# ScalarE's decode steps beside attention keep their place in the queue, at three quarters of the pace

## The chip, the core and the metric

The kernel runs on one core of a Trainium2 chip. The metric is the device time of one execution in microseconds (us). TensorE (PE) multiplies and transposes, and its weight loads (PEld) overlap its matmuls; VectorE (DVE), ScalarE (ACT) and GpSimd (POOL) do elementwise work; SyncE (SP) issues nearly all transfers. Every engine runs its own queue in order: an instruction that waits holds all that stand behind it.

## The reference, cut to what matters

```
x = attention(q, k, v)            # batch 4, heads 8, seq 576, head_dim 64; window of 128, ALiBi bias
x = ((x @ w_a) * (x @ w_b)) @ w_out         # tokens 2304, d_model 512, d_ff 1536
x = f(x @ w_in2) @ w_out2                   # d_ff 2048
# f(h): h if h >= 1; 0 if h <= -1; else (h + 1)**2 / 4
```

q, k and v are 32-bit floats, the five weight matrices 64-bit floats.

## The kernel before

The weights are read as raw 64-bit words in tiles of 128x512 (512 KB) and turned into 32-bit floats on the chip. One such decode is `words` (L518) and a last add: ScalarE writes `e` from the high words (L530) and `up` from the low words (L532); VectorE bounds `e` (L535), shifts it (L539), merges the sign from the high words (L541, the last reader of the raw tile) and adds `up` (L546). There are 68 weight tiles.

Attention runs in rounds. For each block of 64 queries TensorE forms the scores (L348), VectorE reduces them to a maximum (L354), ScalarE takes the exponential (L358), GpSimd normalizes (L363, L369); three rounds later TensorE transposes the probabilities (L380), a copy (mostly ScalarE's, L176) brings them to SBUF as `pt`, and two rounds after that the values are multiplied (L412) and cast into the tiles `x`. Between the rounds TensorE works on the first feed-forward network for half blocks of 256 tokens, with the first four tiles of each weight (gate L593 to L595, down L642).

In the same stretch a third strand decodes 22 more weight tiles ahead of time (`EARLY`): `early_job` (L689) decodes one tile and stores it as 32-bit floats to DRAM (L694, 256 KB), from where it is read back after attention. The main loop at the end of the kernel takes one step of this strand (a job is seven steps) per step of the feed-forward products, `WE` times. The raw words of the coming tiles are loaded by `fetch_next` (L512) until `FETCH` of them are there and unused; there are three raw buffers (two with the tag w64, one w64c). `e` and `up` have two buffers each (`EB`, `UB`), so the first ScalarE step of a job writes into the `e` that the job two before has stored, and waits until that store has landed.

The order in which instructions stand on each engine isn't that of the code. A scheduler goes through the traced program with modelled times and puts each instruction in its engine's queue when the model has its inputs ready. An instruction can be tied to stand behind the one traced just before it on its engine (an order, with no wait on the data).

After attention one visit of the last block of 768 tokens uses the plain weights (L1117, L1148); the other visits use a seven-product form (L1027) on combined weights, that background jobs build from the decoded tiles.

Of the kernel before, what the change touches and what calls it, by code (L numbers as in the profile page):

```python
# [9 lines left out]
F32 = mybir.dt.float32  # L10
# [3 lines left out]
AF = mybir.ActivationFunctionType  # L14
# [12 lines left out]
def attention_and_two_ffns(  # L27
# [12 lines left out]
    nc = tc.nc  # L40
# [53 lines left out]
    YB = 4  # L94
    EARLY = 22
    EFROM = 1
    WE = 1
    HOLD = 3
    PRI = 300
    ET = mybir.EngineType  # L100
# [5 lines left out]
    BG = [(3, 2, 24), (3, 1, 24), (1.5, 1, 19), (2, 1, 12), (3, 1, 0), (3, 1, 0), (2, 1, 0)]  # L106
    VISITS = [(1, 0), (1, 1), (1, 2), (2, 0), (2, 1), (2, 2)]
    FLIP = [0, 1, 0, 0, 1, 0]
    FETCH = 2
    ABS = 'AA'  # L110
    D7 = ((2, 2),)
    GN = 11
# [9 lines left out]
    E_PV = 'V'  # L122
    TQ = 3
    TN = 3
    HP = lambda n: n < HPN
    const = ctx.enter_context(tc.tile_pool(name="const", bufs=1))
    xp = ctx.enter_context(tc.tile_pool(name="xp", bufs=1))
# [41 lines left out]
    def minus(eng, out_, a, hi):  # L169
        eng.tensor_tensor(out_, a, hi.bitcast(F32), ALU.subtract)  # L170
# [298 lines left out]
    def ready(t1):  # L469

        return all(
            t in done for _, t in todo if t[0] * S + PART[int(t[2] >= 2)][0] < t1
        )
# [5 lines left out]
    state = {"w": 0, "credit": 0.0}  # L479
# [24 lines left out]
    def fetch(key, tag="w64"):  # L504
        pool, bw = (later["dec"], WB2) if later else (wdec, WB if tag == "w64" else 1)
        src = source(key)
        raws[key] = raw = pool.tile([P, 4 * P], I64, tag=tag, name="w64", bufs=bw)
        nc.sync.dma_start(
            raw.rearrange("p (c f) -> p c f", f=src.shape[-1]) if len(src.shape) == 3 else raw, src
        )  # L510

    def fetch_next():  # L512

        while coming and len(raws) < FETCH:
            count["e"] = count.get("e", 0) + 1
            fetch(coming.popleft(), "w64" if count["e"] % 3 or FETCH < 2 else "w64c")

    def words(key):  # L518

        pool, be, bu = (later["dec"], EB2, UB2) if later else (wdec, EB, UB)  # L520
        if key not in raws:
            fetch(key)
        raw = raws.pop(key)
        word = raw.bitcast(U32).rearrange("p (n two) -> p n two", two=2)
        lo, hi = word[:, :, 0], word[:, :, 1]
        e = pool.tile([P, 4 * P], U32, tag="e", name="e", bufs=be)
        up = pool.tile([P, 4 * P], U32, tag="up", name="up", bufs=bu)
        ef = e.bitcast(F32)
        if ABS[bool(later)] == "A":
            nc.scalar.activation(ef, hi.bitcast(F32), AF.Abs)  # L530
            yield e, up
        nc.scalar.activation(up, lo, AF.Copy, scale=2.0**-29)  # L532
        yield e, up
        if ABS[bool(later)] == "A":
            nc.vector.tensor_scalar(ef, ef, W64_MIN, W64_MAX, ALU.max, ALU.min)  # L535
        else:
            nc.vector.tensor_scalar(ef, hi.bitcast(F32), W64_MIN, W64_MAX, ALU.abs_max, ALU.min)
        yield e, up
        nc.vector.tensor_scalar(e, e, 5, 2, ALU.logical_shift_left, ALU.logical_shift_right)  # L539
        yield e, up  # L540
        nc.vector.scalar_tensor_tensor(e, hi, 0xC0000000, e, ALU.bitwise_and, ALU.bitwise_or)  # L541
        yield e, up

    def total_bits(dst, e, up):
        shape = (lambda t: t.rearrange("p (a n) -> p a n", a=2)) if len(dst.shape) == 3 else (lambda t: t)
        nc.vector.tensor_tensor(dst, shape(e), shape(up), ALU.add)  # L546

    def w_tile(name):
        return wp.tile([P, 2, 4 * P], F32R, tag="w", name=name)

    def decode(key):
        for e, up in words(key):
            pass
        total_bits(e, e, up)
        t = w_tile("w")
        low = e.bitcast(F32)
        nc.scalar.copy(t[:, 0], low)
        minus(ENG[LESS], t[:, 1], low, t[:, 0])
        wt[key] = t

    def room():
        return WP - state["w"]

    def take(key):
        assert room(), key
        state["w"] += 1

    def give(key):
        state["w"] -= 1

    def pump():
        if not waiting or not room():
            return False
        key = waiting.popleft()
        take(key)
        with tc.high_priority() if HP(order.index(key)) else ExitStack():
            decode(key)
        if not waiting:
            fetch_next()
        return True  # L580
# [95 lines left out]
    V = nc.vector  # L676
# [10 lines left out]
    coming = deque(ahead)  # L687

    def early_job(key):  # L689
        for e, up in words(key):  # L690
            yield
        total_bits(e, e, up)
        early[key] = dram.tile([P, 4 * P], F32, name=f"w32_{key[0]}{key[1]}")
        nc.sync.dma_start(early[key], e.bitcast(F32))  # L694
        fetch_next()
        yield
# [98 lines left out]
    def run(jobs):  # L795

        try:
            return next(jobs[0]) != "no room"
        except StopIteration:
            jobs.popleft()  # L800
            return True
# [24 lines left out]
    less_, plus_ = ALU.subtract, ALU.add  # L826
    def two():
        both = later["dec"].tile([P, 2, QW], F32, tag="x32", name="x32", bufs=1)
        return both[:, 0], both[:, 1]
# [60 lines left out]
    def t_tile(where):  # L890
        if where == "xt":
            return later["xt"].tile([P, 2, 2, QW], F32R, tag="xt", name="xt", bufs=3)
        return xp.tile([P, 2, 2, QW], F32R, tag="x", name="xt", bufs=NB * NC)

    def x_tile(name):
        return xp.tile([P, 2, BW], F32R, tag="x", name=name, bufs=NB * NC)

    def x7_second(b, where):

        t1, t2 = two()  # L900
        xs[b] = [x_tile(f"z{c}") for c in range(NC)]
        if where == "memory":
            parked[2, b] = {q: dram.tile([P, 2, 2, QW], F32, name=f"t2_{b}{q}") for q in (2, 3, 6)}
        else:
            turned[2, b] = {q: t_tile(where) for q in (2, 3, 6)}

        def split(hi, lo, src):
            nc.scalar.copy(hi, src)
            yield
            minus(V, lo, src, hi)  # L910
            yield

        def turn(q, c, src):
            if where != "memory":
                yield from split(*(turned[2, b][q][:, z, c] for z in range(2)), src)
                return
            while not room():
                yield "no room"
            me = ("turned2", b, q, c)
            take(me)  # L920
            t = w_tile("wt")
            yield from split(t[:, 0, :QW], t[:, 1, :QW], src)
            nc.sync.dma_start(parked[2, b][q][:, :, c], t[:, :, :QW].bitcast(F32))
            give(me)

        for c in range(2):
            f = xp.tile([P, 2, BW], F32, tag="x", name="xf", bufs=NB * NC)
            nc.sync.dma_start(f, xf[b][:, c])
            yield
            b11, b12, b21, b22 = f[:, 0, Q1], f[:, 0, Q2], f[:, 1, Q1], f[:, 1, Q2]  # L930
            V.tensor_tensor(t1, b12, b11, less_)
            yield
            V.tensor_tensor(t2, b22, t1, less_)
            yield
            V.tensor_tensor(b12, b22, b12, less_)
            yield
            yield from turn(3, c, t1)
            yield from turn(2, c, t2)
            V.tensor_tensor(t1, b21, t2, less_)
            yield  # L940
            for k in range(2):
                x = xs[b][c + 2 * k]
                yield from split(x[:, 0], x[:, 1], f[:, k])
            yield from turn(6, c, t1)
        made.add((2, b))
        yield
# [475 lines left out]
    def after_attention():  # L1422
# [22 lines left out]
        with tc.manual_schedule(engines=set(MANUAL)) if MANUAL else ExitStack():  # L1445
            for i, v in enumerate(visits):
# [13 lines left out]
                if here == (2, 1):  # L1460
                    jobs_x.append(x7_second(2, "xt"))
                for f in v["fs"]:
                    final = f == v["fs"][-1]

                    def hook(q):
# [8 lines left out]
                        if D7 and here == (2, 1):  # L1474
                            if q == TQ and f != visits[-1]["fs"][-1]:
                                turns[f] = turn_job(v, f)
                            for z in sorted(turns)[:1] if FLIP[i - 1] == 0 else sorted(turns)[::-1][:1]:
                                for _ in range(TN):
                                    if next(turns[z], "end") == "end":
# [43 lines left out]
    for need in products():  # L1523
        if need is not None:
            begun += 1
            while not later and (need > NT or not ready(need)):
                step()
                steps += 1
                if steps % PUMP[0] == PUMP[1]:
                    pump()  # L1530
        if not later and begun >= 0:
            for _ in range(XE):
                if jobs_x:
                    run(jobs_x)
            if begun >= EFROM and ahead and not waiting and not jobs_w:
                jobs_w.append(early_job(ahead.pop(0)))
            for _ in range(WE):
                if jobs_w:
                    run(jobs_w)
        owed += PACE[min(begun, len(PACE) - 1)]  # L1540
        while owed >= 1.0:
            owed -= 1.0
            step()
# [30 lines left out]
```

## Time and profile before

| | us |
|---|---|
| median of three runs | 975.7 (973.14 to 975.98) |
| the profiled execution | 974.94 |
| its span, first to last instruction | 973.2 |
| PE busy in the span | 937.1 (96%) |
| DVE, ACT, POOL busy | 720.6, 565.0, 169.5 |
| decodes ahead of time: ScalarE's first step of the first and of the last | 84.8 and 203.0 |
| TensorE's last product of attention values ends | about 243 |

The busy shares are averages over stages with different limits, so the table only says that TensorE is the engine to look at. Where it stood idle or ran at a lower granted clock is read from the stretches of time, and what it waited for from the waits and the timeline of the same stretch.

### The profile page before, as it was taken

To read this page: it belongs to the slowest core of one execution; us is meant where nothing else is said; L and a number is where in the kernel's file an instruction comes from. 1 tells how busy PE (TensorE), PEld (TensorE's weight loads), DVE (VectorE), ACT (ScalarE), POOL (GpSimd) and SP (SyncE) were. 2 spreads that over 40 slices of the span, in tenths; PEclk is the share of its full clock that TensorE was granted. 3 is DMA by queue.
4 is the path that set the end of the run, shared out by engine and by line. 5 is a ranking of instruction groups with operands and counts; after the bars stand their busy time and mean duration, and the time that the engine had idled before them with its cause. 6 is when DMAs were issued, how large, how long until landed. Compare 5 with 4: busy or idle time off the path is not lost.

```text
span 973.2 us, 18277 instructions
## 1 busy us (share of the span) xinstructions
PE 937.1 (96%) x6397; PEld 874.6 (90%) x6397; DVE 720.6 (74%) x1704; ACT 565.0 (58%) x1346; POOL 169.5 (17%) x311
## 2 busy tenths in 40 slices
PE   4999999899999999999999999999999999999997
PEld 3889889799999899999989999888888888899997
DVE  6698787794944988885677667899876656467886
ACT  6778676664433454353434435788775656586662
POOL 5567444344100000000000000000000000032233
PEclk9999999999999999999999999999999999999999
DMA  9967787830545888798868997876777776587851
GB/s 215 181 147 180 209 218 185 220 98 2 163 156 198 311 311 301 281 365 332 265 225 328 383 364 271 310 247 211 272 285 238 246 241 229 178 269 257 268 185 65
DMA packets 177580, 229.01 MB, mean 235 GB/s; under 512 B 92880, under 2 KB 132048, under 8 KB 177488
## 3 DMA queue, kind: packets, MB, share of 16 engines
q1 hardware_dynamic: 173680, 224.96, 70.9%
q10 hardware_dynamic: 3808, 2.88, 1.0%
q8 instruction: 51, 0.84, 0.3%
q14 instruction: 41, 0.34, 0.1%
HBM read 156.24 MB, written 71.57 MB: 234 GB/s over the span
## 4 chain that ended last, share of the span: by engine, by line
PE 71%; DVE 4%; DMA 3%; issue 1%; ACT 0%; SPq 0%; POOL 0%; DVEq 0%; POOLq 0%
PE mm L1027 32%; PE acc L1209 14%; PE acc L1148 10%; PE acc L1352 5%; PE mm L1117 3%; PE acc L642 1%; DMA xf<-xf 1%; DMA e<-w_b 1%; PE ps_s L348 1%; PE mm L593 1%; PE mm L595 1%; PE ps_o L412 1%; PE mm L594 1%; PE acc L1396 1%; PE ps_t L380 0%
## 5 line engine op out<-in xcount | busy, mean ns | idle before, releaser
L1256 POOL TENSOR_TENSOR h<-h,h 128x384 f32<-128x384 f32 x21 | 23.5, 1118 | 656.0 <-DVE h L1243 647.1
L1027 PE MATMUL mm<-xt,ws 128*128 128x384 f32 x612 | 124.5, 338 | 0.7 <-DVE a L968 0.7
L1027 PEld LDWEIGHTS mm<-xt,ws 128*128 128x128 f32 x612 | 106.8, 188 | 6.0 <-DVE a L968 1.3
L1027 PE MATMUL mm<-z,ws 128*128 128x384 f32 x480 | 97.2, 337 | 0.5 <-DVE h L968 0.5
L1027 PEld LDWEIGHTS mm<-z,ws 128*128 128x128 f32 x480 | 84.4, 188 | 5.3 <-DVE h L968 0.8
L1209 PE MATMUL acc<-ws,gh 128*128 128x512 f32 x252 | 79.0, 394 | 0.0
L369 POOL TENSOR_SCALAR s<-s,ssum 128x192 f32<-128x192 f32 (+2 forms) x144 | 69.8, 498 | 28.9 <-DVE ssum L364 20.9
L358 ACT ACTIVATE s<-s,nmax 128x192 f32<-128x192 f32 (+2 forms) x144 | 62.4, 437 | 16.2 <-DVE nmax L354 15.9
L1027 PE MATMUL mm<-x,ws 128*128 128x384 f32 x348 | 70.7, 338 | 0.3 <-ACT s L1048 0.2
L1148 PE MATMUL acc<-gh,ws 128*128 128x512 f32 (+1 forms) x224 | 65.3, 335 | 0.0
L1027 PEld LDWEIGHTS mm<-x,ws 128*128 128x128 f32 x348 | 61.7, 188 | 3.8 <-ACT s L1048 0.9
L530 ACT ACTIVATE e<-w 128x512 f32<-128x512 f32 x68 | 45.4, 672 | 33.8 <-DMA w_a<-e 6.3
L348 PE MATMUL ps_s<-kt,diag 128*128 128x192 f32 (+2 forms) x288 | 62.1, 337 | 2.0 <-ACT diag L176 0.9
L976 ACT CAST gh<-a 128x384 fp32r<-128x384 f32 x56 | 28.3, 513 | 56.8 <-DVE a L1056 37.9
L968 DVE TENSOR_TENSOR h<-mm,s 128x384 f32<-128x384 f32 x72 | 39.8, 553 | 27.7 <-PE mm L1027 27.6
L1352 PE MATMUL acc<-ws,go 128*128 128x256 f32 x423 | 58.9, 282 | 0.4 <-DVE sum L968 0.4
L593 PE MATMUL mm<-x,w 128*128 128x256 f32 x192 | 57.4, 304 | 0.1
L1352 PEld LDWEIGHTS acc<-ws,go 128*128 128x128 f32 x423 | 56.1, 189 | 1.5 <-DVE sum L968 1.3
L595 PE MATMUL mm<-x,w 128*128 128x256 f32 x192 | 57.0, 298 | 0.1
L532 ACT ACTIVATE up<-w 128x512 uint32<-128x512 uint32 x68 | 45.9, 675 | 19.2 <-DVE e L546 7.5
L594 PE MATMUL mm<-x,w 128*128 128x256 f32 x192 | 56.9, 297 | 0.0
L976 ACT CAST gh<-c 128x384 fp32r<-128x384 f32 x68 | 34.6, 512 | 37.4 <-PE acc L1209 29.9
(153 smaller groups left out, 2519.8 us busy)
## 6 DMA issues: line engine op xcount, KB each, us to landing
ws<-w_ii SPq DMA_DIRECT2D x57, 512.0 KB, 5.5
ws<-w_p SPq DMA_DIRECT2D x48, 512.0 KB, 4.5
ws<-w_ab SPq DMA_DIRECT2D x37, 512.0 KB, 6.3
w_p<-wb SPq DMA_DIRECT2D x30, 512.0 KB, 4.7
w<-in_moe_w_out_dram SPq DMA_DIRECT2D x28, 512.0 KB, 5.0
w_ab<-wb SPq DMA_DIRECT2D x24, 512.0 KB, 3.0
w_ii<-wb SPq DMA_DIRECT2D x24, 512.0 KB, 4.1
w<-in_moe_w_in_dram SPq DMA_DIRECT2D x16, 512.0 KB, 4.7
```

The costliest lines, as they stand in the source:

```text
L348: nc.tensor.matmul(ps[:, z, c : 3 * D], qd[:, i - q0 // D, :], kt[:, (i - 2) * D + c - k0 : (i + 1) * D - k0], start=True, stop=True,)
L358: nc.scalar.activation(at(z, i), at(z, i), AF.Exp, bias=nmax[:, z : z + 1], scale=-1.0, accum_out=ssum[:, z : z + 1],)
L369: ENG[E_N[2 * b + (m >= 2)][z]].tensor_scalar(at(z, i), at(z, i), ssum[:, z : z + 1], 1.0, ALU.mult, ALU.mult)
L532: nc.scalar.activation(up, lo, AF.Copy, scale=2.0**-29)
L593: nc.tensor.matmul(ps, w[:, 0, cs], xh[c], start=(c == 0), stop=False)
L594: nc.tensor.matmul(ps, w[:, 0, cs], xl[c], start=False, stop=False)
L595: nc.tensor.matmul(ps, w[:, 1, cs], xh[c], start=False, stop=(c == NC - 1))
L976: nc.scalar.copy(hi[:, t_], src)
L1027: nc.tensor.matmul(ps, w[:, k, cs], operand(here, q, ci, m), start=q in (0, 1, 3) and ci + n == 0, stop=ci == 1 and n == 2, skip_group_che ...
L1148: nc.tensor.matmul(dst, w[:, i, cs], m[:, t_], start=first and k == 0 and (n < NC or c % 2 == 0), stop=last and k == 2 and (n < NC or c % ...
L1209: nc.tensor.matmul(v["acc"][n], m[:, ss], w[:, i], start=first and k == 0, stop=last and k == 2,)
L1352: nc.tensor.matmul(dst, g[a][:, ss], w[:, b], start=opens and n == 0, stop=closes and n == 2, skip_group_check=True,)
```

## The change

Three settings change. The two ScalarE instructions of a decode beside attention are tied to their place in the traced order of ScalarE (`PIN`; decodes elsewhere aren't). The strand of early decodes takes 0.75 steps instead of 1 per step of the feed-forward products (`WE`). `FETCH` is 3 instead of 2. The settings `XW` and `PINX` stand at values with which the code does what it did.

```diff
--- before.py
+++ after.py
@@ -94,7 +94,6 @@
     YB = 4
     EARLY = 22
     EFROM = 1
-    WE = 1
     HOLD = 3
     PRI = 300
     ET = mybir.EngineType
@@ -106,7 +105,7 @@
     BG = [(3, 2, 24), (3, 1, 24), (1.5, 1, 19), (2, 1, 12), (3, 1, 0), (3, 1, 0), (2, 1, 0)]
     VISITS = [(1, 0), (1, 1), (1, 2), (2, 0), (2, 1), (2, 2)]
     FLIP = [0, 1, 0, 0, 1, 0]
-    FETCH = 2
+    FETCH = 3
     ABS = 'AA'
     D7 = ((2, 2),)
     GN = 11
@@ -122,6 +121,10 @@
     E_PV = 'V'
     TQ = 3
     TN = 3
+    PIN = True
+    WE = 0.75
+    XW = 1
+    PINX = False
     HP = lambda n: n < HPN
     const = ctx.enter_context(tc.tile_pool(name="const", bufs=1))
     xp = ctx.enter_context(tc.tile_pool(name="xp", bufs=1))
@@ -515,7 +518,7 @@
             count["e"] = count.get("e", 0) + 1
             fetch(coming.popleft(), "w64" if count["e"] % 3 or FETCH < 2 else "w64c")
 
-    def words(key):
+    def words(key, pin=lambda ins: ins):
 
         pool, be, bu = (later["dec"], EB2, UB2) if later else (wdec, EB, UB)
         if key not in raws:
@@ -527,9 +530,9 @@
         up = pool.tile([P, 4 * P], U32, tag="up", name="up", bufs=bu)
         ef = e.bitcast(F32)
         if ABS[bool(later)] == "A":
-            nc.scalar.activation(ef, hi.bitcast(F32), AF.Abs)
+            pin(nc.scalar.activation(ef, hi.bitcast(F32), AF.Abs))
             yield e, up
-        nc.scalar.activation(up, lo, AF.Copy, scale=2.0**-29)
+        pin(nc.scalar.activation(up, lo, AF.Copy, scale=2.0**-29))
         yield e, up
         if ABS[bool(later)] == "A":
             nc.vector.tensor_scalar(ef, ef, W64_MIN, W64_MAX, ALU.max, ALU.min)
@@ -687,7 +690,7 @@
     coming = deque(ahead)
 
     def early_job(key):
-        for e, up in words(key):
+        for e, up in words(key, tc.keep_in_program_order if PIN else lambda ins: ins):
             yield
         total_bits(e, e, up)
         early[key] = dram.tile([P, 4 * P], F32, name=f"w32_{key[0]}{key[1]}")
@@ -895,6 +898,9 @@
     def x_tile(name):
         return xp.tile([P, 2, BW], F32R, tag="x", name=name, bufs=NB * NC)
 
+    def pinned(ins):
+        return tc.keep_in_program_order(ins) if PINX else ins
+
     def x7_second(b, where):
 
         t1, t2 = two()
@@ -926,9 +932,10 @@
         for c in range(2):
             f = xp.tile([P, 2, BW], F32, tag="x", name="xf", bufs=NB * NC)
             nc.sync.dma_start(f, xf[b][:, c])
-            yield
+            for _ in range(XW):
+                yield
             b11, b12, b21, b22 = f[:, 0, Q1], f[:, 0, Q2], f[:, 1, Q1], f[:, 1, Q2]
-            V.tensor_tensor(t1, b12, b11, less_)
+            pinned(V.tensor_tensor(t1, b12, b11, less_))
             yield
             V.tensor_tensor(t2, b22, t1, less_)
             yield
@@ -1534,7 +1541,9 @@
                     run(jobs_x)
             if begun >= EFROM and ahead and not waiting and not jobs_w:
                 jobs_w.append(early_job(ahead.pop(0)))
-            for _ in range(WE):
+            state["thin"] = state.get("thin", 0.0) + WE
+            while state["thin"] >= 1.0:
+                state["thin"] -= 1.0
                 if jobs_w:
                     run(jobs_w)
         owed += PACE[min(begun, len(PACE) - 1)]
```

On ScalarE, around the copy of an accumulator to `y` that before makes at 175 us: `w_2930` and `w_3011` are raw tiles of two early decodes before; `pt` are probabilities, `s` scores, `gh` a gated product. Of before:

```order
L358 ACTIVATE s_138,ssum<-s_138,nmax 128x192 x2
L530 ACTIVATE e<-w_2930 128x512
L176 COPY y<-acc 128x512
L622 CAST gh<-a_sb 128x256
L176 COPY pt<-ps_t 128x256
L532 ACTIVATE up<-w_3011 128x512
L358 ACTIVATE s_140,ssum<-s_140,nmax 128x192 x2
L358 ACTIVATE s_134,ssum<-s_134,nmax 128x192
L176 COPY pt<-ps_t 128x384
L530 ACTIVATE e<-w_3011 128x512
```

The same place of the change (there the tiles at hand are `w_2493` and `w_2628`, earlier ones of the 22):

```order
L535 ACTIVATE up<-w_2493 128x512
L625 CAST gh<-a_sb 128x256
L179 COPY pt<-ps_t 128x256
L361 ACTIVATE s_140,ssum<-s_140,nmax 128x192
L179 COPY y<-acc 128x512
L361 ACTIVATE s_140,ssum<-s_140,nmax 128x192
L533 ACTIVATE e<-w_2493 128x512
L179 COPY pt<-ps_t 128x384
L361 ACTIVATE s_134,ssum<-s_134,nmax 128x192
L533 ACTIVATE e<-w_2628 128x512
```

Before, `up` of the next tile stands ahead of `e` of the same tile and right behind the steps of the tile before; now fewer tiles have been decoded by this place.

On SP, in the middle of attention: `L508` (`L511` in the change) loads raw words, `L694` (`L697`) stores a decoded tile, the rest loads q, k and v. Of before:

```order
L694 DMA w_b_2548<-e 128x512
L694 DMA w_o_2669<-e 128x512
L508 DMA w_2671<-in_moe_w_b_dram 128x4x128
L508 DMA w_2738<-in_moe_w_out_dram 128x512
L508 DMA w_2807<-in_moe_w_a_dram 128x4x128
L694 DMA w_a_2736<-e 128x512
L508 DMA w_2930<-in_moe_w_b_dram 128x4x128
```

Of the change:

```order
L511 DMA w_2408<-in_moe_w_a_dram 128x4x128
L697 DMA w_a_2406<-e 128x512
L511 DMA w_2493<-in_moe_w_b_dram 128x4x128
L697 DMA w_b_2491<-e 128x512
L278 DMA qraw<-in_q_dram 32x18x32 x4
L278 DMA kraw<-in_k_dram 32x18x32 x2
L511 DMA w_2628<-in_moe_w_out_dram 128x512
L697 DMA w_o_2626<-e 128x512
```

Loads came in groups of two and three; now each store stands right behind one load, which goes into the raw buffer that the stored tile has just left.

On VectorE, at the end of attention: `L354` (`L357`) is a score reduction, `x_116` and `x_117` the last outputs of attention. Of before:

```order
L364 RECIPROCAL ssum<-ssum 128x1
L170 TENSOR_TENSOR x_116<-ps_o,x_116 128x4x64
L170 TENSOR_TENSOR x_116<-ps_o,x_116 128x5x64
L178 COPY pt<-ps_t 128x384 x2
L178 COPY pt<-ps_t 128x256
L620 TENSOR_TENSOR a_sb<-mm,a_sb 128x256
L866 TENSOR_TENSOR x_4157<-x_106 128x384
L170 TENSOR_TENSOR x_117<-ps_o,x_117 128x4x64
```

Of the change:

```order
L544 SCALAR_TENSOR_TENSOR e<-w_3564,e 128x512
L173 TENSOR_TENSOR x_116<-ps_o,x_116 128x4x64
L181 COPY pt<-ps_t 128x384
L549 ISA e<-e,up 128x1024
L181 COPY pt<-ps_t 128x384
L173 TENSOR_TENSOR x_116<-ps_o,x_116 128x5x64
L623 TENSOR_TENSOR a_sb<-mm,a_sb 128x256
L181 COPY pt<-ps_t 128x256
L538 TENSOR_SCALAR e<-e 128x512
L542 TENSOR_SCALAR e<-e 128x512
L544 SCALAR_TENSOR_TENSOR e<-w_3694,e 128x512
L549 ISA e<-e,up 128x1024
```

Before, no decode stood here; now the last ones of the 22 stand between the last steps of attention.

## Rows read from the trace of the kernel before

**Rows 1.** The page, busy time by engine.

```profile
PE 937.1 (96%) x6397; PEld 874.6 (90%) x6397; DVE 720.6 (74%) x1704; ACT 565.0 (58%) x1346; POOL 169.5 (17%) x311
```

**Rows 2.** Stretches: us, busy us of each engine, PEclk (granted clock), DMA share, GB/s.

```profile
90.00:210.00 120.00, 108.98 (x1139) 103.24 (x1139) 97.33 (x330) 82.48 (x276) 54.09 (x120) 0.96 0.73 195
150.00:160.00 10.00, 10.00 (x73) 9.98 (x73) 7.96 (x33) 7.63 (x26) 3.34 (x8) 0.90 0.64 195
180.00:190.00 10.00, 8.28 (x55) 8.29 (x56) 7.90 (x29) 7.62 (x27) 3.61 (x10) 0.83 0.78 179
205.00:235.00 30.00, 30.00 (x339) 29.42 (x338) 19.47 (x85) 18.02 (x68) 14.76 (x41) 1.00 0.13 38
245.00:305.00 60.00, 60.00 (x382) 58.38 (x381) 38.49 (x77) 21.93 (x46) 3.82 (x3) 1.00 0.48 162
```

**Rows 3.** Waits of PE, 90 to 210 us: us in total, times, longest.

```profile
PE ps_t L380 <- ACT pt L176: 5.4, 3, 3.0
PE ps_o L412 <- ACT pt L176: 2.6, 2, 2.0
PE ps_o L412 <- DVE nmax L354: 0.9, 1, 0.9
```

**Rows 4.** Waits of ACT for transfers, 90 to 210 us.

```profile
ACT e L530 <- DMA w_a<-e: 6.3, 4, 2.3
...
ACT e L530 <- DMA w_o<-e: 4.9, 4, 1.7
...
ACT e L530 <- DMA w<-in_moe_w_a_dram: 3.9, 2, 2.3
ACT up L532 <- DMA w<-in_moe_w_out_dram: 3.0, 1, 3.0
ACT e L530 <- DMA w_b<-e: 2.6, 3, 1.7
ACT e L530 <- DMA w<-in_moe_w_b_dram: 2.4, 1, 2.4
```

**Rows 5.** Timeline of ACT: start, us, instruction, idle before it and releaser.

```profile
179.24 0.67 ACT L532 ACTIVATE up<-w 128x512 uint32<-128x512 uint32 x1 [3.04 <-DMA w<-in_moe_w_out_dram]
...
181.12 0.46 ACT L176 COPY pt<-ps_t 128x384 f32<-128x384 f32 x1
```

**Rows 6.** Timeline of PE at the same time.

```profile
181.72 0.52 PE L380 MATMUL ps_t<-ident,s 128*128 128x128 f32 x3 [2.98 <-ACT pt L176]
```

**Rows 7.** DVE's groups of instructions, 90 to 210 us: count, busy us, mean ns, idle before.

```profile
L354 DVE CUSTOM_DVE_ANT_0 s<-ps_s,bias 128x192 f32<-128x192 f32 (+2 forms) x69 | 20.3, 328 | 1.8 <-PE ps_s L348 1.6
L541 DVE SCALAR_TENSOR_TENSOR e<-w,e 128x512 uint32<-128x512 uint32 x21 | 15.2, 729 | 0.0
L546 DVE CUSTOM_DVE_ANT_0 e<-e,up 128x1024 uint16<-128x1024 uint16 x21 | 14.4, 688 | 0.0
L539 DVE TENSOR_SCALAR e<-e 128x512 uint32<-128x512 uint32 x21 | 11.2, 539 | 0.2
...
L535 DVE TENSOR_SCALAR e<-e 128x512 f32<-128x512 f32 x21 | 9.3, 443 | 13.7 <-ACT e L530 13.5
```

**Rows 8.** Transfers issued at 90 to 210, 172.7, 152.1, 141.3: KB, us to landing.

```profile
w<-in_moe_w_a_dram SPq DMA_DIRECT2D x7, 512.0 KB, 5.4
...
w<-in_moe_w_a_dram SPq DMA_DIRECT2D x1, 512.0 KB, 7.8
...
w_b<-e SPq DMA_DIRECT2D x1, 256.0 KB, 2.0
...
w_a<-e SPq DMA_DIRECT2D x1, 256.0 KB, 5.8
```

**Rows 9.** Timeline of SP: start and length of the issue.

```profile
140.45 0.37 SPq L508 DMA_DIRECT2D w<-in_moe_w_a_dram  x1
141.26 0.34 SPq L694 DMA_DIRECT2D w_a<-e  x1
```

**Rows 10.** Timeline of PE: the first product of the seven-product visits.

```profile
303.35 1.20 PE L1027 MATMUL mm<-x,wb 128*128 128x384 f32 x6
```

## The prediction

> **What bounds the kernel now.** I read the page's busy times first: TensorE is busy 96% of the span [rows 1], so a change that leaves its work alone can gain only where it waits or runs at the lower clock. I looked for these places by stretches of time, ten us each and then the longer ones of [rows 2]. From 205 to 235 and from 245 to 305 us TensorE is busy all the time at full clock. From 90 to 210 us, where the early decodes run beside attention, it is busy 108.98 of 120 us, so it stands idle 11.0 us; the granted clock is 0.96 there, which is 0.04 x 120 = 4.8 us of full-speed time. That is 15.8 us lost, and the most that this change can win in the stretch it touches first. The clock falls behind an idle time: TensorE was idle for 2.98 us until 181.7 [rows 6], and the stretch from 180 to 190 has 0.83; from 150 to 160 it has 0.90 with an engine busy all 10 us [rows 2], after a wait that ended at 148. One such fall is worth (1 - 0.83) x 10 = 1.7 us.
>
> What TensorE waits for is in the waits of the same stretch [rows 3]: mostly `pt`, ScalarE's copy of transposed probabilities (5.4 and 2.6 us), and hardly VectorE (0.9). ScalarE isn't short of time (82.48 busy of 120 us [rows 2]); it is held up. Its own waits [rows 4] say by what: 3.9 + 3.0 + 2.4 = 9.3 us for raw words, and 6.3 + 4.9 + 2.6 = 13.8 us for stores of decoded tiles, whose landing gives the buffer `e` free. Together 23.1 us. One case shows the whole chain: `up` waits 3.04 us for raw words until 179.24, the exponentials and the copy of `pt` queued behind it follow, `pt` starts at 181.12 [rows 5], and TensorE, which had waited 2.98 us for it, goes on at 181.72 [rows 6]. So an instruction that nobody needs soon holds back one that TensorE needs. On average 15.8 us lost for 23.1 us waited are 0.68 us per us; the long waits come through nearly whole, with the clock on top, the short ones less.
>
> **The change part by part.** It adds and removes no arithmetic: 22 early decodes with two ScalarE, four VectorE steps, one load and one store each, before as after. It moves them.
>
> *Raw words three ahead, ScalarE's steps tied to their place.* Before, the scheduler put `e` and `up` where its model had the words landed; in the order of ScalarE `up<-w_3011` stands ahead of the exponentials just because of that, and this is the very instruction that waits at 179.24. Counting through the queues, VectorE makes on average 5 score reductions between its last read of a raw buffer and ScalarE's first read of the words that are loaded into it next, and in the worst case 1; in the change 10 to 11, and never under 5. A reduction comes every 120 / 69 = 1.7 us [rows 7], so the lead grows from 8.7 (at worst 1.7) us to 18 (at worst 8.7) us. A load lands in 5.4 us, at most in 7.8 [rows 8]. All the waits for raw words should go. By the average ratio that is 9.3 x 0.68 = 6.3 us; if they come through whole, as in the case shown, with two falls of the clock, 9.3 + 2 x 1.7 = 12.7 us. They are the longest ones, so I go above the average and take 8.0 us.
>
> *Three quarters of the pace.* The first step of a decode waits for the store of the decode two before. In the queues VectorE's reductions between the last add of that decode and this step are 3.0 on average before (10 of 22 steps have two or fewer), and 5.0 in the change (5 of 22), in us 5.1 and 8.7. That alone would take away half of the 13.8 us. Against it stands the order on SP: now each store follows right behind a load. A store with no load ahead of it landed in 2.0 us; the one issued at 141.26, behind a load of 140.45 [rows 9], took 5.8 us [rows 8]. With 3.8 us more for most stores the wider distance is nearly used up. I take a gain of 1.0 us; the ends are 13.8 x 0.68 = 9.4 us won, and 10 us lost (the third rival).
>
> On SP's queue the page "DMA: Bandwidth & Descriptors" of the Trainium skill, in "Queues, rings and completion order", speaks against the change: descriptors are consumed in ring order, and the one that raises the semaphore lands only after every earlier write of that engine. A store behind a load would then always land after the load, and the third rival would be the forecast (985 us). The trace agrees for the store of 141.26 and its load.
>
> *The decodes that come later.* At 203 us all 22 were begun; now some eight still have VectorE work to do then, four of them wholly within the last attention rounds (three come after the last reduction, between the last copies of `pt`, as the order of VectorE shows). A decode costs VectorE 0.73 + 0.69 + 0.54 + 0.44 = 2.4 us [rows 7]. From 205 to 235 us VectorE is busy 19.47 of 30 us [rows 2]; with 4 x 2.4 = 9.6 us it is 29.1. That is full, where 97.33 of 120 us (81%) was the load at which attention ran from 90 to 210. If it can't do better than 81%, the 30 us become 29.1 / 0.81 = 35.9, 5.9 us more, and with two falls of the clock 9.3 us. If the three rounds between the scores and their transposes cover the lateness, it costs nothing. TensorE hardly waited for VectorE at 81% [rows 3], so I take 2.0 us.
>
> *After attention* nothing follows from a late decode: the first seven-product matmul starts at 303.35 [rows 10], sixty us after attention, and from 245 to 305 VectorE is busy 38.49 of 60 us [rows 2], so 7 us more find room. What TensorE gains by 245 us it keeps.
>
> The sum is -8.0 - 1.0 + 2.0 = -7.0 us against the profiled execution's own 974.94 us (a span of 973.2 with 1.7 us around it): 967.9, forecast 968. The median of the runs is 975.7, 0.8 us above the profiled one; what a measurement of this kernel can tell from no change is about 0.3%, 2.9 us.
>
> **The rivals.**
>
> *Everything comes back.* Neither raw words nor stores hold ScalarE, and the late decodes fit: 974.94 - 15.8 = 959.1. For it: TensorE loses nothing from 205 to 235 us, where there are no decodes. Against it: the decodes are still there, and the stores land later.
>
> *The wait changes its place.* VectorE becomes the bound of the last 30 us of attention; the 9.0 us won before 205 us go into 9.3 us lost behind. Time 975. For it: 29.1 of 30 us. Against it: the scheduler had VectorE's load in its model when it set the order, and VectorE's reductions stand ahead of most decode steps.
>
> *Slower: stores behind loads.* The store of every tile shares the rings with the load issued just ahead, lands 3.8 us later, and the tied first step of the decode two behind waits for it at the head of ScalarE's queue, with exponentials and copies of `pt` behind it. If 10 of the 22 steps wait 3.8 us, ScalarE waits 38 us, TensorE loses 38 x 0.68 = 25.8 instead of 15.8 us: 985. It turns slower than before from 23.1 / 3.8, that is six such steps, on. For it: the order on SP. Against it: five steps, not ten, stand within two reductions (3.5 us) of the add they depend on.
>
> *The change doesn't do what it says*: a tied step follows the one traced before it, and where that one floated up, so may the step. The orders show `e` and `up` later, so this gets no more than a share of "no change".
>
> **How the numbers follow.** The forecast's case 0.56, 963 to 973 us by the ends of its smaller terms; everything back 0.12; no change (the wait changes its place, or the steps still float) 0.16; slower 0.16. Faster by over 0.3% (below 972.8): 0.93 of the forecast's case and the first rival, 0.52 + 0.12 = 0.64. Slower (above 978.6): the third rival and a share of the second, 0.18. Within: 0.18. The range from 959 to 978 holds the forecast's case, the first two rivals and little of the third, some 0.84.
>
> **What would show it.** In the profile of the changed kernel, from 90 to 210 us: no wait of ScalarE's `e` or `up` for raw words over 0.5 us (first term); waits of `e` for the stores of 8 to 15 us in all, each store 4 to 6 us to landing (second); TensorE idle for 3 to 5 us, with one or two falls of the clock. From 205 to 245 us: VectorE busy over 90%, TensorE idle for up to 3 us (third). The visit behind attention starts some 7 us earlier and every later stage by the same. I am wrong if ScalarE still waits for raw words, if the waits for stores exceed 23 us, or if TensorE idles for more than 6 us in the last rounds of attention.

## The result and the profile after

| | before | the change |
|---|---|---|
| median, us (range) | 974.28 (972.74 to 975.98, 5 runs) | 962.80 (962.09 to 963.63, 5 runs) |
| ratio to before, 95% interval | | 0.9879, 0.9860 to 0.9898 |
| profiled execution, us | 974.94 | 962.21 |

The change is faster by 1.2%. The forecast of 968.0 had the direction, and the time lies in its range (959 to 978), 5.2 us below the forecast. The reason that it gave for most of the gain is another matter, as the experiments show. Line numbers of the change are 3 to 8 higher than before (`e` is L533, `up` L535, the reductions L357, the first product of the plain visit L1124).

The page's busy times of the change; they answer to [rows 1]. The work is the same, and what has shrunk is mainly the span around it (TensorE's busy time is 3.3 us less, at a better clock):

```profile
PE 933.8 (97%) x6397; PEld 873.0 (91%) x6397; DVE 722.9 (75%) x1704; ACT 563.8 (59%) x1346; POOL 173.4 (18%) x311
```

Stretches of the change (columns as in [rows 2]):

```profile
0.00:90.00 90.00, 75.52 (x691) 66.06 (x691) 68.06 (x241) 67.91 (x216) 54.47 (x118) 0.92 0.82 176
90.00:210.00 120.00, 116.62 (x1295) 111.93 (x1295) 99.25 (x348) 85.58 (x292) 62.19 (x134) 1.00 0.74 183
180.00:190.00 10.00, 9.62 (x123) 8.80 (x121) 9.56 (x32) 7.69 (x27) 5.41 (x10) 1.00 0.60 176
205.00:235.00 30.00, 30.00 (x382) 28.79 (x381) 25.83 (x84) 19.74 (x62) 14.67 (x32) 1.00 0.38 125
210.00:245.00 35.00, 34.85 (x423) 33.46 (x422) 29.29 (x84) 20.79 (x59) 13.42 (x28) 1.00 0.45 154
245.00:305.00 60.00, 59.90 (x352) 57.77 (x351) 35.41 (x70) 22.13 (x44) 3.05 (x2) 1.00 0.46 161
```

Two of these stretches of before that were not shown, then 70 to 80 us of before and of the change:

```profile
0.00:90.00 90.00, 74.74 (x700) 65.15 (x701) 69.72 (x248) 69.88 (x220) 56.42 (x118) 0.94 0.80 177
210.00:245.00 35.00, 35.00 (x474) 33.73 (x473) 19.42 (x77) 17.87 (x62) 14.87 (x40) 1.00 0.10 26
```

```profile
70.00:80.00 10.00, 8.85 (x81) 8.06 (x82) 8.66 (x30) 7.29 (x23) 5.88 (x12) 0.83 0.71 159
```

```profile
70.00:80.00 10.00, 8.69 (x69) 8.01 (x70) 7.29 (x25) 6.16 (x20) 5.41 (x11) 0.66 0.68 151
```

From 90 to 210 us TensorE stands idle 3.4 instead of 11.0 us, and the granted clock is 1.00 instead of 0.96 (4.8 us back). With 0.15 us lost from 210 to 245, TensorE loses 3.5 instead of 15.8 us in all: 12.3 us, next to the 12.7 us between the two profiled executions. The two don't match to the last us: reckoned in the same way, the change loses 1.0 us more from 0 to 90 us (21.7 against 20.7), and the clock is given to two digits only. Hardly anything changes behind attention in these two executions. The first product of the plain visit, first of before, then of the change (line, engine, tiles, count: ns min/median/max, first and last start in the window):

```profile
L1117 PE MATMUL mm<-x,w x78: 334/334/346, 257.8 to 275.0; 128*128 128x384 f32 x78
```

```profile
L1124 PE MATMUL mm<-x,w x126: 333/335/347, 245.3 to 275.0; 128*128 128x384 f32 x126
```

It starts 12.5 us earlier, and from there to the end of the execution it is 717.1 us before and 716.9 us after.

What TensorE and ScalarE (for transfers) waited for from 90 to 210 us in the change, against [rows 3, 4]:

```profile
PE ps_t L383 <- POOL s L372: 1.4, 1, 1.4
PE ps_t L383 <- ACT pt L179: 0.8, 1, 0.8
PE ps_s L351 <- DVE x L173: 0.7, 1, 0.7
PE ps_o L415 <- ACT pt L179: 0.2, 1, 0.2
...
ACT e L533 <- DMA w_a<-e: 2.7, 2, 1.8
ACT e L533 <- DMA w_b<-e: 2.4, 1, 2.4
ACT e L533 <- DMA w_o<-e: 1.5, 2, 1.1
```

No wait for raw words is left in this stretch, the waits for stores fell from 13.8 to 6.6 us, and TensorE's for `pt` from 8.0 to 1.0. The longest of these waits, in ScalarE's timeline of the change and then in TensorE's, against [rows 5, 6]:

```profile
176.86 0.37 ACT L179 COPY pt<-ps_t 128x256 f32<-128x256 f32 x1 [0.25 <-PE ps_t L383]
179.67 0.68 ACT L533 ACTIVATE e<-w 128x512 f32<-128x512 f32 x1 [2.44 <-DMA w_b<-e]
...
181.69 0.35 ACT L179 COPY pt<-ps_t 128x256 f32<-128x256 f32 x1
```

```profile
182.09 1.66 PE L415 MATMUL ps_o<-pt,v 64*64 64x64 f32 x56 [0.23 <-ACT pt L179]
```

The same kind of wait, 2.44 us at the head of ScalarE's queue, costs TensorE 0.23 us here; before, 3.04 cost 2.98. Wait for wait there is no fixed price. A likely reason, which no run isolates, is how far ahead of TensorE the copies of `pt` are.

VectorE's groups of the same stretch, against [rows 7], say what else is different:

```profile
L357 DVE CUSTOM_DVE_ANT_0 s<-ps_s,bias 128x192 f32<-128x192 f32 (+2 forms) x78 | 22.8, 326 | 5.9 <-PE ps_s L351 5.8
L544 DVE SCALAR_TENSOR_TENSOR e<-w,e 128x512 uint32<-128x512 uint32 x18 | 13.7, 761 | 0.2
L549 DVE CUSTOM_DVE_ANT_0 e<-e,up 128x1024 uint16<-128x1024 uint16 x17 | 13.1, 768 | 1.8 <-ACT up L535 1.5
```

There are 78 reductions instead of 69, so attention gets 13% farther in these 120 us, and 17 to 18 decodes instead of 21. The four that are missing run from 210 to 245 us, where VectorE goes from 19.42 to 29.29 busy of 35 and TensorE stays busy.

### The profile page after: what moved, and what is told of

Read it like the earlier page. It is cut to its first block, busy times and chain, and to the rows that moved or that the text cites. A ratio compares the mean times of both kernels' runs of the same rounds, so it can differ in the third digit from the quotient of the medians.

```text
span 960.4 us, 18289 instructions
## 1 busy us (share of the span) xinstructions
PE 933.8 (97%) x6397; PEld 873.0 (91%) x6397; DVE 722.9 (75%) x1704; ACT 563.8 (59%) x1346; POOL 173.4 (18%) x311
## 4 chain that ended last, share of the span: by engine, by line
PE 76%; DVE 9%; DMA 7%; ACT 4%; issue 2%; POOL 1%; SPq 1%; DVEq 0%; POOLq 0%; ACTq 0%
PE mm L1034 33%; PE acc L1216 14%; PE acc L1155 10%; PE acc L1359 5%; PE ps_s L351 3%; PE mm L1124 2%; PE ps_o L415 2%; PE acc L645 2%; DMA e<-w_b 1%; PE ps_t L383 1%; ACT s L361 1%; PE mm L596 1%; PE mm L597 1%; PE mm L598 1%; DMA w_o<-e 1%
## 5 line engine op out<-in xcount | busy, mean ns | idle before, releaser
L533 ACT ACTIVATE e<-w 128x512 f32<-128x512 f32 x68 | 45.4, 672 | 21.4 <-DMA w<-in_moe_w_out_dram 4.6
L596 PE MATMUL mm<-x,w 128*128 128x256 f32 x192 | 56.6, 299 | 0.1
L597 PE MATMUL mm<-x,w 128*128 128x256 f32 x192 | 56.1, 293 | 0.1
L598 PE MATMUL mm<-x,w 128*128 128x256 f32 x192 | 55.9, 292 | 0.1
L357 DVE CUSTOM_DVE_ANT_0 s<-ps_s,bias 128x192 f32<-128x192 f32 (+2 forms) x144 | 42.6, 328 | 15.2 <-PE ps_s L351 12.6
```

The source lines that it names most:

```text
L533: pin(nc.scalar.activation(ef, hi.bitcast(F32), AF.Abs))
L596: nc.tensor.matmul(ps, w[:, 0, cs], xh[c], start=(c == 0), stop=False)
L597: nc.tensor.matmul(ps, w[:, 0, cs], xl[c], start=False, stop=False)
L598: nc.tensor.matmul(ps, w[:, 1, cs], xh[c], start=False, stop=(c == NC - 1))
```

## The experiments

Three theories stood at the start, one for each setting: the tie and the loads three ahead, each of which could end the waits for raw words, and the pace, which takes decodes out of the crowded stretch and gives stores time to land. In the table, "per decode" is the time between the first ScalarE steps of the 22 early decodes, (last start - first start) / 21 in the profiled execution, and "visit" the start of the plain visit behind attention there.

| kernel | tie | pace | ahead | median, us | ratio (95%) | profiled | per decode | visit |
|---|---|---|---|---|---|---|---|---|
| before | no | 1 | 2 | | | 974.94 | 5.63 | 257.8 |
| only_fetch | no | 1 | 3 | 976.11 | 1.0012 (0.9993 to 1.0030) | 976.40 | 5.61 | 257.1 |
| only_pace | no | 0.75 | 2 | 974.21 | 1.0001 (0.9983 to 1.0019) | 973.70 | 5.65 | 255.2 |
| only_tie | yes | 1 | 2 | 971.82 | 0.9983 (0.9961 to 1.0005) | 977.00 | 5.99 | 260.1 |
| tie_store_pool | yes | 1 | 2 | 970.05 | 0.9949 (0.9929 to 0.9968) | 969.61 | 6.25 | 250.3 |
| pace85 | yes | 0.85 | 3 | 965.09 | 0.9910 (0.9881 to 0.9939) | 969.09 | 6.54 | 251.1 |
| no_fetch | yes | 0.75 | 2 | 964.51 | 0.9900 (0.9871 to 0.9930) | 966.20 | 6.91 | 247.3 |
| the change | yes | 0.75 | 3 | 962.80 | 0.9879 (0.9860 to 0.9898) | 962.21 | 6.79 | 245.3 |
| store_pool | yes | 0.75 | 3 | 965.15 | 0.9900 (0.9877 to 0.9924) | 963.64 | 6.77 | 244.1 |
| after_p6 | yes | 0.75 | 3 | 965.97 | 0.9915 (0.9891 to 0.9940) | 969.07 | 6.89 | 248.9 |
| tie_all | yes | 0.75 | 3 | 972.43 | 0.9966 (0.9948 to 0.9984) | 972.08 | | 252.4 |
| before_e3 | no | 1 | 2 | 985.25 | 1.0098 (1.0074 to 1.0123) | 988.14 | 4.93 | 269.0 |
| tie_e3 | yes | 1 | 2 | 975.66 | 1.0009 (0.9995 to 1.0023) | 977.31 | 5.93 | 257.3 |
| after_e3 | yes | 0.75 | 3 | 967.05 | 0.9914 (0.9898 to 0.9931) | 966.84 | 6.76 | 246.1 |

From "visit" to the end of the profiled execution it is 716.9 to 720.7 us in all of them, while "visit" itself goes from 244 to 269: what they win or lose against before, they do mostly before attention ends. Behind it they differ by up to 3.8 us, though, and that is as much as the kernels near the change differ by: after_e3 starts the visit 0.8 us later than the change and ends 4.6 us later. There is one profiled execution of each kernel, so this part isn't explained here. Profiled executions can lie at the edge of a kernel's runs; that of only_tie is among its latest (967.97 to 977.43), and those of no_fetch, pace85, before_e3, tie_e3 and after_p6 are at the slow end too.

Of the expectations below three were clearly missed: only_tie (966 to 969 by its own theory, 971.8 measured), before_e3 (977 at most, 985.3 measured) and tie_e3 (972 at most by its theories, 975.7 measured). pace85, store_pool and after_p6 came out next to or between the values of their theories.

### One setting at a time

Edits to before, for only_fetch, only_pace and only_tie (before has no tie; the setting is the change's, and each kernel is the code of the change with the other two settings at before's values):

```diff
-    FETCH = 2
+    FETCH = 3
```

> The kernel before with three raw tiles ahead alone. Theory T: 972 to 975 us; the queues show the same distance between the last read of a raw buffer and the next use of it as before (5 reductions on average), since the three buffers were already in use. Theory F: raw waits under 2 us and 965 to 968 us. Theory P: 972 to 975 us.

```diff
-    WE = 1
+    WE = 0.75
```

> The kernel before with three quarters of the pace alone (no tie, two raw tiles ahead). Theory T: without the tie ScalarE's steps float ahead as before whatever the pace of the traced program, so 972 to 975 us, with raw and store waits of 18 us or more in 90 to 210 us. Theory P: most of the gain, 964 to 967 us, waits below 12 us. Theory F: 972 to 975 us.

```diff
-    PIN = False
+    PIN = True
```

> The kernel before with the tie alone (pace 1, two raw tiles ahead). Theory T (the loss comes from ScalarE steps that the scheduler floats ahead of their words; the tie ends it, and the pace only works on top of it): the waits for raw words fall from 9.3 to under 3 us, those for stores stay above 9 us, so half to two thirds of the 11.5 us gain is there: 966 to 969 us. Theory P (too many decodes per us; the pace is what helps): 972 to 975 us. Theory F (the loads come too late; the third raw tile ahead is what helps): 972 to 975 us, raw waits of 6 us or more.

no_fetch, an edit to the change:

```diff
-    FETCH = 3
+    FETCH = 2
```

> The change without its third raw tile ahead (tie and three quarters of the pace, two raw tiles ahead). Theories T and P: 962 to 964 us, the same as the change; the order of TensorE's queue is the same. Theory F: 966 us or more, with raw waits of ScalarE back at 3 us or more.

`FETCH` is nothing: alone it leaves the time as it was, and taken out of the change it moves the ratio from 0.9879 to 0.9900, which the two intervals (0.9860 to 0.9898 and 0.9871 to 0.9930) don't tell apart. The pace alone is nothing either, and the tie alone at most 0.4%. Both together are 1.0% (no_fetch). So the gain is of the two together, not of their sum. Why the pace needs the tie, the first ScalarE steps of the 22 decodes show (columns as for L1124 above) before, with the pace alone, with the tie alone, and in the change:

```profile
L530 ACT ACTIVATE e<-w x22: 658/673/697, 84.8 to 203.0; 128x512 f32<-128x512 f32 x22
```

```profile
L533 ACT ACTIVATE e<-w x22: 658/676/692, 84.8 to 203.4; 128x512 f32<-128x512 f32 x22
```

```profile
L533 ACT ACTIVATE e<-w x22: 654/674/709, 88.3 to 214.0; 128x512 f32<-128x512 f32 x22
```

```profile
L533 ACT ACTIVATE e<-w x22: 649/675/712, 87.8 to 230.4; 128x512 f32<-128x512 f32 x22
```

With the pace alone the last decode begins at 203.4, as before at 203.0: the strand takes its steps later in the code, and the scheduler puts the untied steps as early in ScalarE's queue as it did. Only tied steps keep the slower pace, and then the decodes stretch to 230 us.

Why the tie alone gives so little is in ScalarE's waits for transfers with the tie alone, 90 to 210 us:

```profile
ACT e L533 <- DMA w_b<-e: 6.6, 4, 2.4
ACT e L533 <- DMA w_a<-e: 4.5, 3, 1.6
ACT e L533 <- DMA w_o<-e: 1.2, 1, 1.2
```

The waits for raw words are all gone, with two ahead as with three, just as the forecast said. But 12.3 us of waits for stores stay, TensorE is still idle 8.7 us there at a clock of 0.97, and a new loss stands where there was none before, at 212 us (ScalarE's timeline with the tie alone, then TensorE's):

```profile
210.75 0.67 ACT L533 ACTIVATE e<-w 128x512 f32<-128x512 f32 x1 [2.33 <-DMA w_a<-e]
211.32 0.66 ACT L535 ACTIVATE up<-w 128x512 uint32<-128x512 uint32 x1
211.89 0.45 ACT L179 COPY pt<-ps_t 128x384 f32<-128x384 f32 x1
```

```profile
212.48 0.83 PE L383 MATMUL ps_t<-ident,s 128*128 128x128 f32 x3 [3.15 <-ACT pt L179]
```

In that execution TensorE is busy 32.52 of 35 us from 210 to 245, with a clock of 0.95. Idle time and clock from 90 to 245 add up to 8.7 + 3.6 + 2.5 + 1.8 = 16.6 us, where before lost 15.8.

### The pace in between

```diff
-    WE = 0.75
+    WE = 0.85
```

> The change with a pace of 0.85 steps instead of 0.75, all else as in the change. Theory D (what counts is how many reductions lie in the queues between the last add of a decode and the tied step two decodes later): that distance is 3.7 here (9 of 22 steps at two or fewer), close to the 3.4 (9) of the tie alone and far from the 5.0 (5) of the change; so ScalarE waits 10 to 12 us for stores between 90 and 210 us, and the time is 970 to 972, as with the tie alone. Theory Q (what counts is the share of ScalarE and of the transfers that decodes take per us): the gain grows evenly with the pace taken away, 0.85 lies three fifths of the way from 971.8 to 963, store waits 8 to 9 us, time 966 to 967.

The time, 965.1, agrees with a gain that grows with the pace taken away (971.8, 965.1 and 962.8 at paces 1, 0.85 and 0.75, 5.99, 6.54 and 6.79 us per decode), not with the counts in the queues, which put it next to the tie alone. The waits for stores in its profiled execution (969.1, the slowest of its four) fit the counts, though: 5.1 + 3.9 + 2.8 = 11.8 us. With nearly the waits of the tie alone (12.3) TensorE lost less, 8.2 us idle at a clock of 1.00. The waits alone don't fix the loss.

### A third buffer of `e`

Three buffers of `e` instead of two take away what makes a step wait for a store. Room for it came from the buffers of `pt` (6 instead of 7).

The edit makes before_e3 of before, tie_e3 of only_tie and after_e3 of the change; after_p6 is the change with the second half of it alone:

```diff
-    EB = 2
+    EB = 3
...
-    PT = 7
+    PT = 6
```

> The kernel before with a third buffer for e (and six for the transposed probabilities), no tie, full pace. Theory S: the stores' part of the waits goes (13.8 us to under 5), but steps that float ahead wait for raw words instead, since they may now float one decode further: raw waits rise above 9.3 us and the time stays within 970 to 977 us. Theory D: no change, 973 to 976 us. If the stores alone were the cost, 965 to 968 us.

> The tie at full pace, with a third buffer for e (EB 3; to make room, six buffers instead of seven for the transposed probabilities). After only_tie (raw waits 0, store waits of 12.3 us in 90 to 210 us, 971.8 us) theory S: the store of the decode two before is what ScalarE's first step waits for at full pace, and the slower pace's worth is that it has landed by then. With a third e the store waits go below 3 us and the time to 961 to 965 us without the slower pace. Theory D: what the slower pace takes away is VectorE's and ScalarE's own work per us, so that TensorE waits less for reductions and casts; then the store waits go but the time stays at 968 to 972 us, with TensorE still waiting for pt, x and nmax for 6 us or more.

> The change with a third buffer for e (and six for the transposed probabilities). Theory S: its store waits (6.6 us of ScalarE in 90 to 205 us) go, TensorE's idle time there falls from 2.7 us by one or two: 960 to 962.5 us. Theory D: 962 to 964 us, no difference. If six buffers for the probabilities hurt: 965 us or more.

> The change with PT 6 instead of 7 and two buffers of `e` as in the change: the other half of what made room for a third `e`. Theory W (the 4 us that the kernels with a third `e` lose before 90 us come from the smaller PT): TensorE is busy 71 to 72 us of the first 90 instead of 75.5, and the time is 967 to 968. Theory X (they come from the third `e` itself, that lets the first decodes run closer together): 75 us or more of the first 90, time 962 to 964.

All three with a third `e` lose time first in a stretch that the theories didn't speak of. TensorE from 0 to 90 us, in after_e3 and in after_p6:

```profile
0.00:90.00 90.00, 71.54 (x631) 62.88 (x631) 67.35 (x231) 66.94 (x208) 53.10 (x111) 0.94 0.80 171
```

```profile
0.00:90.00 90.00, 75.90 (x697) 65.25 (x698) 69.63 (x241) 68.34 (x217) 55.74 (x118) 0.94 0.82 177
```

So the 4 us of busy time missing there come with the third `e`, not with fewer `pt` alone. With the clock reckoned in (0.94 in after_e3 and 0.92 in the change, 5.4 and 7.2 us of 90) they are worth 2.2 us. For the whole time the two halves can't be told apart: after_p6 is 965.97 at a ratio of 0.9915, after_e3 967.05 at 0.9914. Its own profiled execution (969.07, 3 us above its median) loses 5.5 us from 90 to 210 us, where the change loses 3.4, so fewer `pt` may cost something too, elsewhere. From 90 to 210 us after_e3 has no wait for stores or raw words at all (one of 2.4 us for raw words comes later), and from 90 to 245 it loses 2.2 us instead of 3.5. Without the tie (before_e3) the third `e` lets the scheduler push the decodes closer, 4.93 us each, and it is the slowest of all, with 13.5 us of waits for raw words. The case that says most is tie_e3, though it has one `pt` buffer fewer and its profiled execution is among its slowest: ScalarE waits only 4.9 us for stores from 90 to 210, less than in the change, and TensorE still loses 6.5 us idle and 4.8 us of clock. What it waits for there is no longer ScalarE's `pt` but VectorE:

```profile
PE ps_o L415 <- DVE nmax L357: 4.1, 2, 2.0
PE ps_t L383 <- POOL s L372: 0.8, 2, 0.5
PE ps_s L351 <- DVE nmax L357: 0.7, 1, 0.7
PE ps_t L383 <- ACT pt L179: 0.6, 1, 0.6
```

The reading that fits is that at 5.93 us per decode the decodes are too dense for this stretch, whichever engine shows it; how much of these waits comes from fewer `pt` wasn't run.

### The stores on a queue of their own

The edit makes tie_store_pool of only_tie and store_pool of the change:

```diff
-        nc.sync.dma_start(early[key], e.bitcast(F32))
+        nc.gpsimd.dma_start(early[key], e.bitcast(F32))
```

> The tie alone at full pace (two raw words ahead), with the early store issued from GpSimd's queue instead of SyncE's, so that it no longer stands behind a load in one queue. Theory B (with the tie alone the gain is lost since stores land late behind loads): the stores land in about 2 to 3 us instead of 3.9 to 4.5, ScalarE's waits for stores fall from 12.3 to 5 us or less, and the time is 964 to 967. Theory D (the distance in the queues is too short whatever the landing): waits for stores stay at 9 us or more and the time is 970 to 973. If GpSimd is held up by the store that it issues, TensorE waits for `s` by more than 3 us and the time is above 974.

> The change with the early store issued from GpSimd's queue instead of SyncE's. Theory B (stores land late behind loads): the 6.6 us that ScalarE still waits for stores between 90 and 205 us go to 3 or less, the stores land in 2 to 3 us, TensorE's 3.4 us idle of 90 to 210 fall by half, time 960 to 962. If what is left isn't from the stores: 963 as the change. If GpSimd's normalizing waits behind the store that it issues: TensorE's waits for `s` grow from 1.4 to over 4 us and the time is 966 or more.

The stores' transfers in tie_store_pool and, below, in only_tie (84 to 250 us: queue of the issue, count, KB, median us to landing):

```profile
w_a<-e POOLq DMA_DIRECT2D x8, 256.0 KB, 4.1
w_b<-e POOLq DMA_DIRECT2D x7, 256.0 KB, 5.4
w_o<-e POOLq DMA_DIRECT2D x7, 256.0 KB, 3.3
```

```profile
w_a<-e SPq DMA_DIRECT2D x8, 256.0 KB, 4.0
w_b<-e SPq DMA_DIRECT2D x7, 256.0 KB, 4.5
w_o<-e SPq DMA_DIRECT2D x7, 256.0 KB, 3.9
```

They landed no sooner from a queue without loads. An issue takes longer on GpSimd (median 0.59 us, against 0.34 on SyncE), which is too little to hide a gain of 1 to 2 us. The theory that they are late because they stand behind loads in one queue falls. The 970.05 of tie_store_pool, with 8.9 us of waits for stores, is near what the distance in the queues let expect; the order of this kernel is a little wider than that of only_tie, 6.25 us per decode, between only_tie and pace85, as its time is. store_pool, tried to beat the change, waits 4.6 us for stores, has less idle time from 90 to 210 (2.35 us) than the change and the earliest visit of all, but 1.4 us of idle time from 210 to 245 and 2.6 us more behind attention: 0.9900, no better. Nothing run beat the change.

### The tie for the first twelve tiles too

An edit to the change, in `decode` of the tiles that the first feed-forward network needs at once:

```diff
-        for e, up in words(key):
+        for e, up in words(key, tc.keep_in_program_order):
```

> The change with the tie for the first twelve decodes too (those of the plain weights, up to 90 us), where ScalarE still waits for raw words before 90 us and TensorE idles for about 2 us from 60 to 90 us and falls to 0.66 of the clock in 70 to 80. Theories S and D alike: the raw waits before 90 us go, 958 to 962 us; if the tie delays weights that the products wait for, 964 us or more.

It gives back most of the gain, and in the stretch that it touches: TensorE is busy 72.83 us of the first 90 at a clock of 0.89 (75.52 and 0.92 in the change); from 90 to 210 it is as good as the change (117.54 of 120 us, clock 1.00). The likely reason is that tied decodes come later, and the first weights are needed soon; when each weight arrived wasn't compared.

## Why the prediction was right, and where its reason was not

*What bounds the kernel.* Right: the 15.8 us lost from 90 to 210 us were the place, 12.3 of them came back, and the stages behind took as long as before (717.1 and 716.9 us).

*Raw words three ahead, steps tied: 8.0 us taken.* This step failed: "By the average ratio that is 9.3 x 0.68 = 6.3 us; if they come through whole [...] 12.7 us". The waits for raw words did all go, but 9.3 us of them gone brought 3.0 us with the tie alone (974.86 to 971.82, with an interval that includes no change), and three ahead brought none: only_fetch has 11.7 us of such waits. (The tie with three ahead at full pace wasn't run.) The step priced a removed wait at the average loss per us waited (0.68) or above. The runs show that this ratio isn't a price: 12.3 us lost from 90 to 210 for 12.3 waited with the tie alone, 11.3 for 4.9 in tie_e3, 3.4 for 6.6 in the change. Where one wait goes while the decodes stay as dense, the steps run into the next limit, first the stores, then VectorE.

*Three quarters of the pace: 1.0 us taken.* Mis-sized: on top of the tie it is worth 971.8 - 964.5 = 7.3 us. The waits for stores fell by half, as the counting of distances said, and the 3.8 us per store that the forecast set against it were too much at both ends. Its 2.0 us are those of one store, with no load of raw words shortly ahead of it but a small load of `v` (issued at 150.27, landed 2.5 us later); the medians of before from 90 to 210 us are 2.3 to 3.7. And in the change stores landed in 3.6 to 4.7 us (medians) instead of 5.8: those of `w_b` and `w_o` some 2 us later than before, those of `w_a` as before. Of before, then of the change, answering to [rows 8]:

```profile
w_a<-e SPq DMA_DIRECT2D x8, 256.0 KB, 3.7
...
w_b<-e SPq DMA_DIRECT2D x7, 256.0 KB, 2.3
w_o<-e SPq DMA_DIRECT2D x7, 256.0 KB, 2.8
```

```profile
w_a<-e SPq DMA_DIRECT2D x6, 256.0 KB, 3.6
w_b<-e SPq DMA_DIRECT2D x6, 256.0 KB, 4.7
w_o<-e SPq DMA_DIRECT2D x5, 256.0 KB, 4.6
```

What the step did not price at all is that fewer decodes share ScalarE and VectorE with each round of attention.

*The decodes that come later: 2.0 us lost.* It was nothing. VectorE is busy 25.83 of 30 us from 205 to 235, not 29.1: (25.83 - 19.47) / 2.4 = 2.6 decodes' worth, where the forecast had four. TensorE is busy all 30 us. At 86% VectorE did not hold it up; the lower end of that term (no cost, covered by the rounds between scores and transposes) was the right one.

*The signs to look for.* No raw wait: so it is. Waits for stores 8 to 15 us: 6.6. TensorE idle 3 to 5 us: 3.4, with no fall of the clock instead of one or two. VectorE over 90% from 205 to 245: 34.22 of 40 us, 86%. TensorE idle up to 3 us there: 0.15. The visit 7 us earlier: 12.5.

*The rivals.* "Everything comes back" (959.1) is the nearest to the time in its mechanism, 3.1 us below it. "Stores behind loads" did not come about in the change: five steps waited, 6.6 us, not ten for 38. The store of 141.26 in the kernel before did land behind its load (147.1 and 146.2 us), but no long waits followed from that order in the change. "The wait changes its place" did not come about either; with the tie alone a wait did move to the last rounds (3.15 us at 212 us), but for ScalarE's `pt`, not for VectorE. Steps that still float are what the pace alone shows, not the change.

The three terms came out at about -3.0, -7.3 and 0 us instead of -8.0, -1.0 and +2.0: off by some +5, -6 and -2 us (measured less forecast). The first two errors nearly cancel, which was luck, and so the whole was off by less than 5 (11.5 us gained for 7.0). The forecast was right by a bound (the 15.8 us) more than by its parts; the 962.8 lie between its own case (963 to 973) and the first rival.

*What stays open.* How much of the gain is shorter waits and how much less crowding. In most runs wider spacing and shorter waits come together. Where they part, the loss follows the waits badly: from 90 to 210 us tie_e3 loses 11.3 us with 4.9 us of waits for stores, pace85 8.2 with 11.8, and tie_all 2.5 with 8.3. That speaks for the crowding, but by one profiled execution each, so it is not shown. That a spacing of 6.8 us without the tie would do the same was not run; pace 0.75 did not give that spacing without it.

## What to carry to other kernels

When background work shares engines with a stretch that has no room and a stretch behind it has (VectorE 81% here, 55% there), spread the work; the wait that the profile names is only the first limit it meets. A slower pace in the code is worth nothing where a scheduler may move the steps forward again, so look first whether the first and the last of them really start elsewhere in the trace. Try the parts of a change apart: two settings that gave 0.2% and nothing gave 1.0% together.

## What the runs showed of the hardware

A 256 KB store landed in 3.3 to 5.4 us (medians) from a queue of its own, as it did behind loads (3.9 to 4.5), against 2.0 us for one with no load of raw words shortly ahead of it [rows 8]. The Trainium skill, "DMA: Bandwidth & Descriptors", in "Queues, rings and completion order", says that each transfer engine takes turns between the queues it has work for, packet by packet; by that alone the store need not wait for a load in another queue to end, and it might have landed sooner. But the write that raises the semaphore, which the prediction drew on, lands by the same section only after every earlier write of that transfer engine across its queues, so another queue doesn't wholly part a store from the loads. No run here shows that a store lands sooner from a queue of its own; the busy share of the transfer engines from 90 to 210 us was 0.73 to 0.75 in these kernels.

The clock is worth as much as some waits. In the change the granted clock is 1.00 from 90 to 210 us, with no wait of TensorE longer than 1.4 us; but from 70 to 80 us it is 0.66 (0.50, the lower of its two levels, all the time from 74 to 78 us), where before had 0.83, behind idle times of 0.96 and 0.46 us against 0.62 and 0.53 at the same place. That is 1.7 us given away at almost the same busy time (8.69 and 8.85 of 10 us).
